# A causal convolution on TensorE: from groups of four phases to groups of eight, with the order of three engines written out by hand

## The chip, the core and the metric

The kernel runs on one core of one Trainium2 chip. A core has five engines that each take their instructions in order: TensorE (PE; its weight loads are listed as PEld), VectorE (DVE), ScalarE (ACT), GpSimd (POOL) and SyncE (SP). SP does no arithmetic here: it issues DMA transfers. ACT and POOL can issue DMAs too, and such an issue stands in the same queue as their computation. The metric is the device time of one execution in microseconds (us). Less is better.

## The reference: what is computed

The input `x` has 2 batches of 16000 tokens with 144 channels, in bf16. Fifteen taps at a distance of two tokens, each a 144 x 288 matrix, make a causal convolution; half of its 288 outputs goes through a tanh, the other half through a sigmoid, the product is multiplied by a 144 x 144 matrix.

```python
pad = (K - 1) * dil                       # K = 15, dil = 2
xp = jnp.pad(x, ((0, 0), (pad, 0), (0, 0)))
h = jnp.einsum('btc,cd->btd', xp[:, pad:pad + T, :], w[0])
for i in range(1, K):
    off = pad - i * dil
    h = h + jnp.einsum('btc,cd->btd', xp[:, off:off + T, :], w[i])
z = jnp.tanh(h[..., :D]) * _sigmoid(h[..., D:])
return z @ w_o
```

## The kernel before

**Layout.** TensorE contracts over at most 128 partitions, and there are 144 channels. So `x` is loaded transposed (channel on the partition, token along the row) in two pieces: `xn` holds channels 0 to 127, `xb` channels 16 to 143. The 16 channels left over (128 to 143) are copied out of `xb` eight times into one tile `rx`, each copy four tokens later than the one before. One matmul over `rx` so does the left-over channels of eight taps. Each batch is cut into chunks of 2048 tokens (16 chunks in all; the last of a batch is shorter). A chunk is loaded by `load_chunk` (L136): two transposing DMAs and eight copies, all on SP, with three buffers.

**Splitting over phases.** In the transposed layout a matmul takes 128 tokens with a step, as weights (`lhsT`), and the 288 outputs of one tap as the moving operand. Output tokens are sorted by their position modulo eight. A unit `unit_k4` (L334) makes four phases of 128 tokens each, at a step of eight: 512 tokens. It doesn't do fifteen taps for each of four phases. As in fast FIR algorithms it splits the filter into even and odd taps twice, and pays for fewer matmuls with sums: differences of the input (`en` = x shifted by 2 minus x, `fn` the same by 4, `gn` the same of `en` by 4) and of the weights (`s_main`, `ss`, `nso`, `aes`, `aos`, `nw2`) are made first. Then nine groups of four or five matmuls (41 in all, each 128x128 against 128x288) go to nine PSUM banks: `a1`, `a2`, `a3`, `c1`, `b1`, `b2`, `b3`, `c2`, `c3`. All matmuls are recorded on one line, L319 in `mm_group`. ACT copies `a1`, `c1` and `b1` to SBUF; DVE makes `q2 = a2 + a1`, `q3 = a3 + a1`, four sums `u0` to `u3` of two SBUF tiles (L360, L362, L368, L370), and four sums of a `u` with `b2`, `b3`, `c2`, `c3` (L373 to L382) into `y`.

**Gate and projection.** `gate` (L321) takes tanh and sigmoid on ACT and their product on DVE. Products go to DRAM (`zs_dram`), come back transposed as `zta` and `ztb` (72 channels each) by two transposing DMAs on SP, and `emit_outproj` (L299) multiplies them by the two halves of `w_o`: two matmuls with 144 columns for 128 tokens (L307, L308), copied out by ACT (L309). In the last chunk PE itself transposes (`emit_zside_pe`, L253). What 2048-token chunks leave over in a batch is done by `unit_k2` (two phases, 26 matmuls for 256 tokens) and `unit_std` (no splitting, 17 matmuls for 128 tokens).

**What sets the order.** The Tile scheduler orders the instructions of each engine; manual dependencies (`dma_T`, `dma_plain`) keep transposing and plain DMAs from running at the same time. Six PSUM banks serve the groups (`ps_acc`), two the projection (`ps_out`). The differences of the next chunk (`derive_steps`, each a DVE instruction over 2078 columns) are spread over the units of the present chunk, and so is the projection of the chunk before.

Of the kernel before, what the change touches and what calls it, by code (L numbers as in the profile page):

```python
# [15 lines left out]
def kernel(  # L16
# [6 lines left out]
):  # L23
    nc = tc.nc
    P = 128
    B, T, D = x.shape
    K = w.shape[0]
    D2 = w.shape[2]
    assert D2 == 2 * D and w.shape[1] == D
    CM = 128  # L30
    CR = D - CM
    assert CR == 16 and K == 15
    DH = D // 2
    KV = 8
    KO = 7
    NG = 8
    BOFF = D - P
    HTOK = 32
    assert T % P == 0 and T >= 4 * P
    dep_sync = mybir.DependencyInfo(mybir.DependencyClass.Sync, mybir.DependencyReason.DATA)  # L40
    dep_order = mybir.DependencyInfo(mybir.DependencyClass.NoSync, mybir.DependencyReason.SCHED_ONLY)

    KIND_TOK = {"k4": 8 * P, "k2": 4 * P, "std": P}

    def mk_items():
        items = []
        t = 0
        for kind in ("k4", "k2", "std"):
            n = KIND_TOK[kind]
            while T - t >= n:  # L50
                items.append((kind, t))
                t += n
        assert t == T
        return items

    CTOK = 2 * KIND_TOK["k4"]

    def mk_chunks():
        items = mk_items()
        groups = []  # L60
        i = 0
        while i < len(items):
            j = i
            span = 0
            while j < len(items) and span + KIND_TOK[items[j][0]] <= CTOK:
                span += KIND_TOK[items[j][0]]
                j += 1
            rest = sum(KIND_TOK[it[0]] for it in items[j:])
            if rest < KIND_TOK["k4"]:
                j = len(items)  # L70
            groups.append(items[i:j])
            i = j
        res = []
        for g in groups:
            t_a = g[0][1]
            t_b = g[-1][1] + KIND_TOK[g[-1][0]]
            res.append((g, t_a, t_b))
        return res

    def chunk_geom(t_a, t_b):  # L80
        if t_a == 0:
            R = min((t_b + 15) // 16 * 16, T)
            return R, 0, HTOK
        R = (t_b - t_a + HTOK + 15) // 16 * 16
        return R, t_b - R, 0

    chunk_list = mk_chunks()
    WB = 0
    SLOT = 0
    for (_, t_a, t_b) in chunk_list:  # L90
        R, t_lo, jlo = chunk_geom(t_a, t_b)
        assert t_lo >= 0 and t_lo + R <= T
        WB = max(WB, jlo + R)
        SLOT = max(SLOT, t_b - t_a)
    WB = (WB + 15) // 16 * 16
    SLOT = (SLOT + 15) // 16 * 16
    ZPAD = 16
    all_chunks = [(b, items, t_a, t_b) for b in range(B) for (items, t_a, t_b) in chunk_list]
    NCH = len(all_chunks)

    const = ctx.enter_context(tc.tile_pool(name="const", bufs=1))
    xa_pool = ctx.enter_context(tc.tile_pool(name="xa", bufs=3))
    xd_pool = ctx.enter_context(tc.tile_pool(name="xd", bufs=2))
    cp_pool = ctx.enter_context(tc.tile_pool(name="cp", bufs=3))
    y_pool = ctx.enter_context(tc.tile_pool(name="y", bufs=3))
    act_pool = ctx.enter_context(tc.tile_pool(name="act", bufs=2))
    z_pool = ctx.enter_context(tc.tile_pool(name="z", bufs=4))
    zt_pool = ctx.enter_context(tc.tile_pool(name="zt", bufs=2))
    os_pool = ctx.enter_context(tc.tile_pool(name="os", bufs=4))
    ztd_pool = ctx.enter_context(tc.tile_pool(name="ztd", bufs=2))  # L110
    ps_acc = ctx.enter_context(tc.tile_pool(name="ps_acc", bufs=6, space=bass.MemoryType.PSUM))
    ps_out = ctx.enter_context(tc.tile_pool(name="ps_out", bufs=2, space=bass.MemoryType.PSUM))
    dram = ctx.enter_context(tc.tile_pool(name="dram", bufs=1, space=bass.MemoryType.DRAM))

    fence_plain = []
    last_T = [None]

    def dma_T(out_ap, in_ap):
        ti = nc.sync.dma_start_transpose(out=out_ap, in_=in_ap)  # L119
        for prev in fence_plain:  # L120
            tc.add_manual_dep(ti.ins, prev, dep_sync, reason="dma batching")
        fence_plain.clear()
        if last_T[0] is not None:
            tc.add_manual_dep(ti.ins, last_T[0], dep_order, reason="dma batching")
        last_T[0] = ti.ins.name
        return ti

    def dma_plain(eng, out_ap, in_ap, track=True):
        di = eng.dma_start(out=out_ap, in_=in_ap)  # L129
        if last_T[0] is not None:  # L130
            tc.add_manual_dep(di.ins, last_T[0], dep_sync, reason="dma batching")
        if track:
            fence_plain.append(di.ins.name)
        return di

    def load_chunk(ci, cp_eng):  # L136
        b, items, t_a, t_b = all_chunks[ci]
        R, t_lo, jlo = chunk_geom(t_a, t_b)
        xn = xa_pool.tile([P, WB], BF16, name="xn")
        xb = xa_pool.tile([P, WB], BF16, name="xb")  # L140
        rx = xa_pool.tile([P, WB], BF16, name="rx")
        wv = jlo + R
        if jlo > 0:
            nc.gpsimd.memset(xn[:, 0:jlo], 0.0)
            nc.gpsimd.memset(xb[:, 0:jlo], 0.0)
        nc.gpsimd.memset(rx[:, 0:HTOK], 0.0)  # L146
        for (dst, c0) in ((xn, 0), (xb, BOFF)):
            src = bass.AP(x.tensor, x[b, t_lo, c0].offset, [[D, R], [1, P]])
            dma_T(dst[:, jlo:jlo + R], src)
        engs = cp_eng if isinstance(cp_eng, list) else [cp_eng]  # L150
        lasts = {}
        for g in range(NG):
            e_ = engs[g % len(engs)]
            lasts[id(e_)] = dma_plain(e_, rx[g * CR:(g + 1) * CR, 4 * g:wv], xb[P - CR:P, 0:wv - 4 * g],
                                      track=False)
        for l_ in lasts.values():
            fence_plain.append(l_.ins.name)
        return dict(xn=xn, rx=rx, joff=jlo - t_lo, wv=wv, has_k4=any(it[0] == "k4" for it in items))

    def derive_steps(cur):  # L160
        xn, rx, wv = cur["xn"], cur["rx"], cur["wv"]
        steps = []

        def s_en():
            en = xd_pool.tile([P, WB], BF16, name="en")
            nc.vector.tensor_tensor(out=en[:, 0:wv - 2], in0=xn[:, 2:wv], in1=xn[:, 0:wv - 2], op=ALU.subtract)  # L166
            cur["en"] = en

        def s_re():
            re = xd_pool.tile([P, WB], BF16, name="re")  # L170
            nc.vector.tensor_tensor(out=re[:, 0:wv - 2], in0=rx[:, 2:wv], in1=rx[:, 0:wv - 2], op=ALU.subtract)  # L171
            cur["re"] = re

        def s_fn():
            fn = xd_pool.tile([P, WB], BF16, name="fn")
            nc.vector.tensor_tensor(out=fn[:, 0:wv - 4], in0=xn[:, 4:wv], in1=xn[:, 0:wv - 4], op=ALU.subtract)  # L176
            cur["fn"] = fn

        def s_gn():
            en = cur["en"]  # L180
            gn = xd_pool.tile([P, WB], BF16, name="gn")
            nc.vector.tensor_tensor(out=gn[:, 0:wv - 6], in0=en[:, 4:wv - 2], in1=en[:, 0:wv - 6], op=ALU.subtract)  # L182
            cur["gn"] = gn

        steps = [s_en, s_fn, s_gn, s_re] if cur["has_k4"] else [s_en, s_re]
        cur["derived"] = True
        return steps

    def derive_chunk(cur):
        for f in derive_steps(cur):  # L190
            f()

    loaded = {}

    def ensure_chunk(ci, cp_eng=None):
        if ci < NCH and ci not in loaded:
            loaded[ci] = load_chunk(ci, cp_eng or nc.sync)

    w_all = const.tile([CM, K, D2], BF16)
    for qi, (t0, t1) in enumerate(((0, 4), (4, 8), (8, 12), (12, K))):  # L200
        dma_plain([nc.sync, nc.scalar][qi % 2], w_all[:, t0:t1, :], w[t0:t1, 0:CM, :].rearrange("k c d -> c k d"))

    def W(i):
        return w_all[:, i, :]

    ident = const.tile([P, P], BF16)
    make_identity(nc, ident[:])

    warm = const.tile([P, 1], F32)
    nc.gpsimd.memset(warm[:], 0.0)  # L210
    nc.scalar.activation(out=warm[:], in_=warm[:], func=ACT.Sigmoid)

    we_r = const.tile([NG * CR, D2], BF16)
    wo_p = const.tile([KO * CR, D2], BF16)
    dma_plain(nc.scalar, we_r[:], w[0:K:2, CM:D, :])
    dma_plain(nc.scalar, wo_p[:], w[1:K:2, CM:D, :])
    wo_sb = const.tile([DH, 2, D], BF16)
    dma_plain(nc.sync, wo_sb[:], w_o.rearrange("(h r) e -> r h e", h=2))

    zs_dram = dram.tile([NCH, SLOT + ZPAD, D], BF16, name="zs_dram")  # L220
    zpad_sb = const.tile([NCH, ZPAD * D], BF16)
    nc.gpsimd.memset(zpad_sb[:], 0.0)
    dma_plain(nc.sync, zs_dram[:, SLOT:SLOT + ZPAD, :].rearrange("c r d -> c (r d)"), zpad_sb[:])
# [29 lines left out]
    def emit_zside_pe(z_ap, ne, dst_ap):  # L253
        ps = ps_acc.tile([P, 512], F32, name="zt_ps", tag="acc")[0:DH, :].bitcast(BF16).rearrange(
            "p (e h m) -> p e h m", e=2, h=2)[:, :, :, 0:P]
        for e in range(ne):
            for h in range(2):
                nc.tensor.transpose(ps[:, e, h, :], z_ap(e)[:, h * DH:(h + 1) * DH], ident[:])  # L258
# [258 lines left out]
```

## Time and profile before

| | before |
|---|---|
| time, median of 3 runs (lowest to highest) | 390.22 us (389.55 to 390.4) |
| profiled execution: span from first to last instruction | 387.7 us |
| time that the page gives beside the span | none; the median of the runs is 2.5 us above the span |
| PE busy | 364.3 us, 3124 matmuls |
| DVE busy | 331.1 us, 753 instructions |
| ACT busy | 189.4 us, 448 instructions |
| POOL busy | 4.7 us, 28 instructions |
| moved by DMA | 60.27 MB, mean 155 GB/s |

Busy time counts the computing instructions of an engine from their start to their end; ends of matmuls are modelled, and one matmul overlaps the next, so that a mean duration (286 ns for 288 columns) says less than the distance between two starts. A group of instructions is given as line, engine, operation, `out<-in`, shapes, count, total busy time and mean duration of one; behind the bar stands how long the engine sat idle just before them, and for what. `L319` is line 319 of the kernel above. `ACTq` and `SPq` are issues of DMAs by these queues.

### The profile page before, as it was taken

To read this page: it belongs to the slowest core of one execution; us is meant where nothing else is said; L and a number is where in the kernel's file an instruction comes from. 1 tells how busy PE (TensorE), PEld (TensorE's weight loads), DVE (VectorE), ACT (ScalarE), POOL (GpSimd) and SP (SyncE) were. 2 spreads that over 40 slices of the span, in tenths; PEclk is the share of its full clock that TensorE was granted. 3 is DMA by queue.
4 is the path that set the end of the run, shared out by engine and by line. 5 is a ranking of instruction groups with operands and counts; after the bars stand their busy time and mean duration, and the time that the engine had idled before them with its cause. 6 is when DMAs were issued, how large, how long until landed. Compare 5 with 4: busy or idle time off the path is not lost.

```text
span 387.7 us, 8354 instructions
## 1 busy us (share of the span) xinstructions
PE 364.3 (94%) x3124; PEld 354.1 (91%) x3124; DVE 331.1 (85%) x753; ACT 189.4 (49%) x448; POOL 4.7 (1%) x28
## 2 busy tenths in 40 slices
PE   0669999999999999999999999999999999999995
PEld 0468998999999999999989999999999999999984
DVE  3489999998989999899859989999898989897651
ACT  4223445446454644546444454546545454654544
POOL 3000000000000000000000000000000000000000
PEclk9999999999999999999999999999999999999998
DMA  5865794596858859598798979696877969590602
GB/s 154 141 124 104 153 188 87 149 213 170 182 150 156 165 164 191 161 171 175 174 175 132 203 155 198 164 218 137 189 149 174 166 162 200 129 148 30 188 16 110
DMA packets 143475, 60.27 MB, mean 155 GB/s; under 512 B 131275, under 2 KB 133819, under 8 KB 143435
## 3 DMA queue, kind: packets, MB, share of 16 engines
q1 hardware_dynamic: 132764, 40.87, 58.7%
q10 hardware_dynamic: 10671, 18.88, 13.6%
q8 instruction: 24, 0.39, 0.4%
q14 instruction: 16, 0.13, 0.1%
HBM read 1.29 MB, written 18.03 MB: 50 GB/s over the span
## 4 chain that ended last, share of the span: by engine, by line
PE 71%; DVE 13%; DMA 5%; ACT 5%; issue 3%; ACTq 1%; SPq 1%; DVEq 0%
PE out_ps L307 4%; PE out_ps L308 3%; DMA xb<-in_x_dram 3%; ACT th L324 2%; ACTq L129 1%; DMA rx<-xb 1%; ACT sg L325 1%; PE v_ps L319 1%; DMA wo_p<-in_w_dram 1%; DVE en L166 1%; PE yo_ps L319 1%; DVE fn L176 1%; DVE re L171 1%; PE ye_ps L319 1%; SPq L119 1%
## 5 line engine op out<-in xcount | busy, mean ns | idle before, releaser
L319 PEld LDWEIGHTS <-gn 128*128 128x128 bf16 x900 | 116.0, 144 | 0.5 <-issue 0.3
L319 PEld LDWEIGHTS <-en 128*128 128x128 bf16 x540 | 67.0, 141 | 3.5 <-issue 2.6
L319 PEld LDWEIGHTS <-fn 128*128 128x128 bf16 x480 | 61.2, 144 | 2.6 <-DVE fn L176 1.8
L319 PEld LDWEIGHTS <-xn 128*128 128x128 bf16 x302 | 36.1, 136 | 13.6 <-DMA xn<-in_x_dram 11.8
L307 PE MATMUL out_ps<-wo_sb,zta 72*128 72x144 bf16 x237 | 38.7, 226 | 1.5 <-ACT os_2884 L309 0.7
L308 PE MATMUL out_ps<-wo_sb,ztb 72*128 72x144 bf16 x237 | 37.9, 227 | 0.0
L319 PEld LDWEIGHTS <-re 112*128 112x128 bf16 x248 | 35.3, 143 | 1.2 <-DVE re L171 1.1
L308 PEld LDWEIGHTS <-ztb 72*128 72x128 bf16 x237 | 31.4, 143 | 5.2 <-issue 2.3
L307 PEld LDWEIGHTS <-zta 72*128 72x128 bf16 x237 | 32.8, 144 | 0.1
L171 DVE TENSOR_TENSOR re<-rx 128x2078 bf16<-128x2078 bf16 (+1 forms) x16 | 19.3, 1206 | 5.8 <-DMA rx<-xb 5.8
L166 DVE TENSOR_TENSOR en<-xn 128x2078 bf16<-128x2078 bf16 (+1 forms) x16 | 19.3, 1205 | 1.9 <-DMA xn<-in_x_dram 1.9
L319 PEld LDWEIGHTS <-rx 128*128 128x128 bf16 (+1 forms) x128 | 18.0, 142 | 1.9 <-DMA rx<-xb 1.8
L182 DVE TENSOR_TENSOR gn<-en 128x2074 bf16<-128x2074 bf16 (+1 forms) x16 | 19.3, 1206 | 0.1
L176 DVE TENSOR_TENSOR fn<-xn 128x2076 bf16<-128x2076 bf16 (+1 forms) x16 | 19.3, 1204 | 0.0
L319 PE MATMUL a_192<-ss,xn 128*128 128x288 bf16 x4 | 1.2, 447 | 11.8 <-DMA xn<-in_x_dram 11.8
L229 DVE COPY s_main<-w_all 128x288 bf16<-128x288 bf16 x1 | 0.2, 234 | 6.6 <-DMA w_all<-in_w_dram 6.6
L260 DVE COPY zt_sb<-zt_ps 72x512 bf16<-72x512 bf16 (+1 forms) x7 | 2.6, 394 | 3.7 <-PE zt_ps L258 3.7
L146 POOL MEMSET rx<- 128x32 bf16 x16 | 1.8, 122 | 302.3 <-PE a_449 L319 33.3
L319 PE MATMUL v_ps<-s_main,xn 128*128 128x288 bf16 x32 | 4.7, 286 | 0.0
L319 PE MATMUL h_ps<-w_all,xn 128*128 128x288 bf16 x30 | 4.7, 286 | 0.0
L319 PE MATMUL yo_ps<-w_all,en 128*128 128x288 bf16 x32 | 4.6, 286 | 0.0
L319 PE MATMUL ye_ps<-wo_neg,en 128*128 128x288 bf16 x28 | 4.4, 286 | 0.0
(1922 smaller groups left out, 987.8 us busy)
## 6 DMA issues: line engine op xcount, KB each, us to landing
rx<-xb SPq DMA_DIRECT2D x14, 65.0 KB, 2.7
rx<-xb SPq DMA_DIRECT2D x14, 64.8 KB, 2.6
rx<-xb SPq DMA_DIRECT2D x14, 64.5 KB, 4.0
rx<-xb SPq DMA_DIRECT2D x14, 64.2 KB, 2.8
rx<-xb SPq DMA_DIRECT2D x13, 64.9 KB, 2.9
rx<-xb SPq DMA_DIRECT2D x13, 64.6 KB, 2.6
rx<-xb SPq DMA_DIRECT2D x13, 64.4 KB, 3.0
rx<-xb SPq DMA_DIRECT2D x13, 64.1 KB, 3.2
```

The costliest lines, as they stand in the source:

```text
L119: ti = nc.sync.dma_start_transpose(out=out_ap, in_=in_ap)
L129: di = eng.dma_start(out=out_ap, in_=in_ap)
L166: nc.vector.tensor_tensor(out=en[:, 0:wv - 2], in0=xn[:, 2:wv], in1=xn[:, 0:wv - 2], op=ALU.subtract)
L171: nc.vector.tensor_tensor(out=re[:, 0:wv - 2], in0=rx[:, 2:wv], in1=rx[:, 0:wv - 2], op=ALU.subtract)
L176: nc.vector.tensor_tensor(out=fn[:, 0:wv - 4], in0=xn[:, 4:wv], in1=xn[:, 0:wv - 4], op=ALU.subtract)
L182: nc.vector.tensor_tensor(out=gn[:, 0:wv - 6], in0=en[:, 4:wv - 2], in1=en[:, 0:wv - 6], op=ALU.subtract)
L260: nc.vector.tensor_copy(out=sb[:, 0:ne], in_=ps[:, 0:ne])
L307: nc.tensor.matmul(po[:, e, :], lhsT=ck["zta"][0:DH, sl], rhs=wo_sb[:, 0, :], start=True, stop=False)
L308: nc.tensor.matmul(po[:, e, :], lhsT=ck["ztb"][0:DH, sl], rhs=wo_sb[:, 1, :], start=False, stop=True)
L319: nc.tensor.matmul(ps[:, 0:D2], lhsT=l, rhs=r, start=(i == 0), stop=(i == n - 1))
L324: nc.scalar.activation(out=th[:, 0:ne, :], in_=y_ap[:, :, 0:D], func=ACT.Tanh)
L325: nc.scalar.activation(out=sg[:, 0:ne, :], in_=y_ap[:, :, D:D2], func=ACT.Sigmoid)
```

## The change

The convolution, the gate and the projection are written anew. The pieces:

- **Windows and octets.** Each batch is cut into 8 windows of 2000 tokens, of which each is computed as 2048 (128 rows of 16 phases), so there is one kind of unit. A window makes two octets (`rho` 0 and 1): eight phases of 128 tokens at a step of 16. There are 32 octets, and neither `unit_k2` nor `unit_std`.
- **A third level of splitting.** The five groups `A1`, `A2`, `A3`, `B1`, `C1` (class `Leaf`) are split over two phases each: `common` makes two matmuls, ACT copies that partial sum from one PSUM bank into a second one, and `private` accumulates two matmuls on top in either bank (of difference tiles `d8`, `d48`, `d28`), `rest` one more where left-over channels belong. The four groups `b2`, `b3`, `c2`, `c3` (`direct`) are as before, done for two phases each. An octet has 34 matmuls of leaves and 38 of direct products, all with 288 columns.
- **Who adds.** The sums of two SBUF tiles (before: `u0` to `u3` on DVE) are on GpSimd, four per octet, each over two phases (128 x 576 values, fp32), written into `y`. DVE adds `b2` to `c3` from PSUM onto `y`. It makes `q2`, `q3` as before.
- **Input differences.** Seven instead of four per window. Four of the seven (`d8`, `d4`, `d48`, `d28`) only make the columns that are read: runs of 2 or 4 with gaps.
- **Products and projection.** Products are stored as `zm` (channels 0 to 127 of eight phases) and `zr` (the other 16 channels of eight phases side by side). The projection makes three groups of PSUM per octet, each one matmul of the left-over channels of two or three phases against a block-diagonal `wo_bd` and one matmul with 144 columns per phase. Two stores per octet are issued on ACT, two transposing loads on SP; the projection lags two octets.
- **Order.** PE, ACT and DVE run in the order in which the program is written. In the loop the leaves of octet n+1 lie between the direct products of octet n, the gate's second half of octet n-1 and the projection of octet n-2. Five PSUM banks are for leaves and three for direct products and projection. Input tiles have two buffers instead of three; window w+2 is loaded into the buffers of w.
- **Start.** Twenty matmuls over zeros run first; all four loads of `w_all` are on ACT, behind the load of its function table; three small weight loads and three preparations of weights are on GpSimd.

The core of the diff (of the removed side only the tails that the text speaks of; the functions themselves are printed above):

```diff
-        u1 = cp_pool.tile([P, D2], F32, name="u1")
-        nc.vector.tensor_tensor(out=u1[:], in0=c1s[:], in1=q2[:], op=ALU.add)
...
-        mm_group(c3, [(st(gn, -8 * j), W(4 * j)) for j in range(4)] + [(st(re, 4), we_r[:])])
-        nc.vector.tensor_tensor(out=y_sb[:, 3, :], in0=c3[:, 0:D2], in1=u3[:], op=ALU.add)
...
+        return [sub("d8", "x", 8, 0, 8, 2), sub("d4", "x", 4, 0, 4, 2), sub("d48", "d4", 8, 0, 4, 2),
+                sub("d2", "x", 2), sub("d28", "d2", 8, 6, 8, 4), sub("d24", "d2", 4), sub("re", "rx", 2)]
...
+    warm = const.tile([P, 1], F32)
+    nc.vector.memset(warm[:], 0.0)
+    nc.scalar.activation(out=warm[:], in_=warm[:], func=ACT.Sigmoid)
+    zero = const.tile([P, 512], BF16)
+    nc.vector.memset(zero[:], 0.0)
+    for i in range(NWARM):
+        t = ps_leaf.tile([P, 512], F32, name="lf", tag="lf")
+        nc.tensor.matmul(t[:], lhsT=zero[:, 0:P], rhs=zero[:], start=True, stop=True)
...
+    add(bc[:], wq[:, :, 0], wq[:, :, 1], nc.gpsimd)
...
+        def common(self):
+            sig, dsig, off, v, e, o, rem = self.a
+            self.ts = [bank(), bank()]
+            for j in range(2):
+                mm(self.ts[0], st(sig, off - 16 * j), v(j), j == 0, j == 1)
+            nc.scalar.copy(out=self.ts[1][:, 0:D2], in_=self.ts[0][:, 0:D2])
+
+        def private(self, i):
+            sig, dsig, off, v, e, o, rem = self.a
+            f, o_ = ((e, off - 8), (o, off))[i]
+            for j in range(2):
+                mm(self.ts[i], st(dsig, o_ - 16 * j), f(j), False, rem is None and j == 1, True)
...
+        def eoBC(self, leaf, name, u, v, op):
+            t = self.new(name)
+            for i in range(2):
+                leaf.private(i)
+                nc.scalar.copy(out=t[:, i, :], in_=leaf.rest(i)[:, 0:D2])
+            for k, q in ((u, self.q2), (v, self.q3)):
+                nc.gpsimd.tensor_tensor(out=self.y[:, k::4, :], in0=q[:], in1=t[:], op=op)
+
+        def direct(self, k, off, f, n, rem, op, phases):
+            d24 = self.s["d24"]
+            rsig, roff, rw, rows = rem
+            for i in phases:
+                ps = ps_dir.tile([P, 512], F32, name="dir", tag="dir")
+                for j in range(n):
+                    mm(ps, st(d24, off + 8 * i - 8 * j), f(j), j == 0, False)
+                mm(ps, st(rsig, roff + 8 * i, rows), rw, False, True)
+                nc.vector.tensor_tensor(out=self.y[:, k + 4 * i, :], in0=self.y[:, k + 4 * i, :], in1=ps[:, 0:D2], op=op)
...
+    def z_by_dma(slot, zm, zr):
+        zt = zt_pool.tile([P, 9, P], BF16, name="zt")
+        nc.scalar.dma_start(out=zm_dram[slot], in_=zm[:].rearrange("p r c -> p (r c)"))
+        nc.scalar.dma_start(out=zr_dram[slot], in_=zr[:].rearrange("p r c -> p (r c)"))
+        nc.sync.dma_start_transpose(out=zt[:, 0:8, :], in_=zm_dram[slot])
+        nc.sync.dma_start_transpose(out=zt[:, 8, :], in_=zr_dram[slot])
+        return zt
...
+        if o:
+            o.A1.common()
+        if d:
+            d.b2()
+        if o:
+            o.A2.common()
+            o.eoA1()
+        if p:
+            p.act(1)
+        if d:
+            d.b3((0,))
+        if o:
+            o.A3.common()
+            o.eoA(o.A2, "q2", ALU.subtract)
+        if d:
+            d.b3((1,))
+        if p:
+            p.mult(1)
+        if o:
+            o.B1.common()
+            o.eoA(o.A3, "q3", ALU.add)
+        if p:
+            z_side(n - 1)
+        pre()
+        if d:
+            d.c2((0,))
+        project()
+        if d:
+            d.act(0)
+            d.c2((1,))
+        pre()
+        if o:
+            o.C1.common()
+            o.eoBC(o.B1, "b1s", 0, 2, ALU.subtract)
+        project()
+        if d:
+            d.c3((0,))
+            d.mult(0)
+        if o:
+            o.eoBC(o.C1, "c1s", 1, 3, ALU.add)
+        pre()
+        if d:
+            d.c3((1,))
+        project()
+        pre()
```

Here `o` is octet n+1, `d` octet n, `p` octet n-1; `pre()` emits one input difference of the next window, `project()` one group of the projection of octet n-2, `act` the tanh and sigmoid of four phases, `mult` their two products (`zm` and `zr`), `eoA1` the `private` parts of `A1` with a copy of each to SBUF, `eoA` those of `A2` or `A3` with the DVE sum into `q2` or `q3`.

## The prediction

> **What bounds the kernel now.** I read the page's table of engines first, then the chain of work that ended last, then busy time by stretch, and then one unit of the steady part in the timeline. All times are in us.
>
> ```profile
> PE 364.3 (94%) x3124; PEld 354.1 (91%) x3124; DVE 331.1 (85%) x753; ACT 189.4 (49%) x448; POOL 4.7 (1%) x28
> ...
> PE 71%; DVE 13%; DMA 5%; ACT 5%; issue 3%; ACTq 1%; SPq 1%; DVEq 0%
> ```
>
> PE is busy nearly always and carries 71% of the chain. DVE, with 85%, is close behind; ACT has half its time free, POOL nearly all.
>
> ```profile
> 0.00:23.11 23.11, 7.50 (x41) 5.53 (x42) 9.10 (x14) 7.00 (x9) 2.97 (x13) 1.00 0.65 133
> 23.11:200.00 176.89, 174.06 (x1483) 169.83 (x1482) 164.44 (x370) 86.70 (x205) 1.11 (x10) 1.00 0.77 162
> 200.00:360.00 160.00, 159.35 (x1385) 157.64 (x1384) 144.31 (x335) 82.74 (x200) 0.62 (x5) 1.00 0.76 161
> 380.70:387.70 7.00, 2.92 (x36) 2.27 (x33) 1.18 (x4) 3.00 (x10) 0.00 (x0) 0.86 0.30 111
> ```
>
> The columns are: stretch, length, busy time (and count) of PE, PEld, DVE, ACT, POOL, then clock, DMA share, GB/s. The start of 23.1 does only 41 matmuls' work, the tail of 7.0 next to none. Between them the granted clock is full and PE works.
>
> ```profile
> 205.61 0.65 PE L319 MATMUL a_3321<-ss,xn 128*128 128x288 bf16 x4
> 205.89 0.45 DVE L373 TENSOR_TENSOR y_3243<-b_3289,u_3285 128x288 f32<-128x288 f32 x1
> 206.25 0.45 DVE L376 TENSOR_TENSOR y_3243<-b_3295,u_3287 128x288 f32<-128x288 f32 x1
> ...
> 207.46 0.69 ACT L324 ACTIVATE th<-y_3243 128x576 bf16<-128x576 f32 x1 [0.76 <-DVE y_3243 L382]
> ...
> 208.06 0.67 ACT L325 ACTIVATE sg<-y_3243 128x576 bf16<-128x576 f32 x1
> ...
> 210.64 0.65 PE L319 MATMUL a_3401<-ss,xn 128*128 128x288 bf16 x4
> ```
>
> From `a_3321` to `a_3401` a unit of 41 matmuls takes 5.03: 0.1227 per 288-column matmul. What counts is this distance of starts, not the mean duration. In the same way DVE takes 0.37 for a sum over 288 values, ACT 0.60 for 576, and ACT copies of 288 stand 0.30 apart (`c1s` to `b1s`). PE's 144-column projections stand 0.0625 apart.
>
> **PE's work, before and after.** Before: 2598 matmuls of 288 columns (per batch 30 x 41 + 2 x 26 + 17) x 0.1227 = 318.8, 500 of 144 columns x 0.0625 = 31.3, transposes 2: 352 in all. After: 32 octets x 72 x 0.1227 = 282.7; projection per octet 8 x 0.0625 plus 1152 columns at the 288-column rate (0.49), 0.99 x 32 = 31.7. In all 314.4: 38 less, or 9.82 per octet. The octets' 2.4% of tokens computed twice are in it. Weights read at a step of 16 cost the same, I assume: steps of 1, 4 and 8 all show 0.122 to 0.123 here, and a weight load fits into the 0.0625 of a projection matmul. A clear loss would show as longer distances.
>
> **Start.** Before, PE's first matmul waits to 11.85 for `xn` and the second unit starts at 23.11. After, `xb` and `xn` are issued first on SP; `xn` landed 4.2 after its issue here, so it is there at about 8. The four loads of `w_all` now queue on ACT behind the table load (1.28), 0.55 an issue, and landed after 4.2 to 4.5: about 7.5 to 10. Then DVE does 14 preparations: at 1.15 for 2078 values (0.554 ns each) and about 0.07 apiece they add to 9.6, ending at 17 to 19.5. Four `q` sums (1.5) and the round trip of `B1` and `C1` over ACT (2) follow: the loop starts at 20.5 to 23, I take 22. By then the 34 leaf matmuls of octet 0 are done (4.2 of the 314.4). The upper end is 27, if POOL's `bc` (2304 values; 5.1 at the rate below) holds DVE up all the while. The twenty matmuls over zeros end before 12 even at the distance of 0.245 per 288 columns that the first four matmuls of the profile show, in time in which PE waits anyway.
>
> **Tail.** After the last direct product: DVE 0.45, tanh and sigmoid 1.3, products 0.55, nine transposes and three DVE copies (0.41 each) 1.5, six projection groups with ACT copies 2.5, issue and landing of one store of 590 KB (288 KB took 2.1 to 4.3): about 10. Bounds: 7, as before, and 13.
>
> So with PE never waiting in the loop: 22 + 310.2 + 10 = 342 of span. The page gives the profiled execution its span alone, 387.7; the median of the runs, 390.22, is 2.5 above it, and with that I get 345. Each us that PE waits per octet adds 32. Call it s: **time = 344.7 + 32 s**.
>
> **What s holds, per octet of 9.82.** ACT: 11 copies x 0.30, 4 gate halves x 0.60, projection copies 1.2, 2.5 DMA issues x 0.34: 7.75. DVE: 12 sums x 0.37 = 4.44, products 0.88, differences (3.5 per octet; 4930 values x 0.554) 2.73: 8.05. If runs of 2 or 4 go at half that rate, 1815 values cost 1.0 more: 9.05. Before, DVE had 10.4 per 1024 tokens (two units of 11 x 0.37, four differences of 1.15 to every four units), 3.0 of it in the eight `u` sums that move to POOL. So DVE has 1.77 to spare.
>
> POOL: four sums of 576 values. No sum of tiles ran on POOL, so two rows bound it: 2304 values were set in 2.01, which gives 0.50 for 576; the selection of 128x128 in `ident` took 0.28, which gives 1.27. I take 1.27, since it reads and writes SBUF as a sum does and the other only writes. 5.1 per octet fits into 9.82. A sum written after `B1`'s copies, at about 9.0, ends at 10.3; its first reader is `b2`'s add in the next octet at 10.7.
>
> The trace never shows POOL reading SBUF while DVE works. If neither holds up the other, the loss c on DVE is 0 (a gain is excluded: nothing of DVE gets shorter). If each sum holds up one DVE instruction by its whole length, c is 5.1. DVE's instructions that work on SBUF alone (products, differences) are 3.6 of its 8.05, or 45%; that share of 5.1 is 2.3. I take c = 2.3: 0.5 over the slack of 1.77.
>
> The Trainium skill ("SBUF — State Buffer", section "Who interferes with whom") states that a DVE instruction with two SBUF inputs and a GpSimd instruction that reads SBUF exclude each other for whole instructions. No row here shows it. It speaks against this change: taken at its hardest, with c = 5.1, s would be 3.3 and the time 450; by the trace's rows alone c may as well be 0.
>
> ACT has a chain of its own. Counting from an octet's start, PE ends the first projection group at 6.15; ACT copies it until 6.85, then does `act(0)` until 8.1, then `C1`'s bank copy until 8.6; PE wants `C1`'s private matmuls at 8.45. That is a wait of 0.2. Queued in front on ACT are the two stores of `z_side`, which wait for DVE's `mult(1)` (done at 5.2): if DVE is a us late there, PE is too. This overlaps with DVE's lateness; together I take **s = 0.5**.
>
> **Moved steps with one answer each.** SP per window: two loads (2.1 each), eight `rx` copies (6.9 to 8.0), two long and two short transposes (half of 2.1 and less): 15 of 20.6; before, 16 of 22. The load of window w+2 is queued behind the `A1` matmuls of w and lands some 6 later; DVE reads it 15 after. Without that cover every us of lateness would hold DVE up once per window, 0.5 on s. A product's way through DRAM (store landing 2 to 4, transpose 4) is 8 of the 10.4 that two octets of lag leave.
>
> **The sum.** 344.7 + 32 x 0.5 = 361, against 390.2: 29 less, of 38 that PE saves.
>
> **Rivals.**
> - *PE alone bounds:* c below 1.8, ACT's chain in time: 343 to 349. For it: PE waited only 0.65 in the stretch from 200 to 360. Against: then one engine had slack; now DVE, ACT and PE all stand at 79 to 100%.
> - *DVE becomes the bound without deciding the sign:* strided differences at half rate (9.05) with c of 1.7 to 2.1, s = 0.9 to 1.4: 373 to 389. For it: no row shows a difference over short runs. Against: 3.0 of sums has left DVE.
> - *POOL's sums decide, slower than before:* between `mult(0)` and the next `mult(1)` the sums run back to back, and every product and difference there waits for one. From c = 3.2 (63% of the sums' time) s passes 1.42 and the gain is gone. At c = 3.8, three sums of four, s = 2.0: 409; at the end 450. For it: four of DVE's eight SBUF-only instructions lie in that stretch. Against: `c3` and `b2` adds read PSUM and lie between them.
> - *The change doesn't do what it says:* excluded for the count of matmuls; for POOL, the same as the one above.
>
> **How the numbers follow.** Forecast 0.52 (349 to 373), PE alone 0.13, DVE in between 0.13, POOL decides 0.18, below 343 0.02, and 0.02 within 0.2% of the time before, about what a measurement of this kernel can tell from no change. Faster: 0.80; slower: 0.18. The range from 343 to 386 leaves out the slower cases and holds 0.8. The start's upper end (+5) and the tail's (+3) lie inside.
>
> **What the new profile would show.** PE: 2685 matmuls with 288 columns still 0.123 apart; the loop from about 22; 10.3 per octet. POOL sums of 1.27, and products or differences on DVE longer than 0.37 and 1.23, or late, just where a sum runs. PE's waits named after `C1`'s copy or after DVE's adds. I am wrong if POOL's sums take 2 and more, if distances of matmuls grow with the step of 16, or if the wait of an octet sits on a DMA.

## The result, and the profile after

The changed kernel takes **445.6 us** (444.69 and 446.45; two further runs took 461.35 and 468.87) against 389.88 beside it: slower, by a factor of **1.143 [1.140, 1.146]**. The profiled execution took 444.69, with a span of 442.9. Runs more than 1.5% above the fastest of the same kernel are left out of every time and ratio here, and as the traces of e4 and e11 come from such runs, only single rows of them are read.

First the page's table of engines and its chain, to be held against 94%, 85%, 49%, 1% and a chain of 71% PE:

```profile
PE 346.3 (78%) x2685; PEld 315.5 (71%) x2685; DVE 376.4 (85%) x636; ACT 238.2 (54%) x581; POOL 231.4 (52%) x163
...
PE 41%; DVE 33%; issue 10%; DMA 8%; ACT 4%; SPq 1%; POOL 1%; DVEq 0%; ACTq 0%
```

PE has fewer matmuls, as planned, and is no longer what ends last. DVE has 117 instructions fewer than before and is busy 45 us longer; POOL's sums are busy 213 us (104.3 + 109.1 below) where 128 sums of 1.27 would have made 163. Busy time by stretch (columns as before: stretch, length, PE, PEld, DVE, ACT, POOL, clock, DMA share, GB/s):

```profile
0.00:37.92 37.92, 14.97 (x55) 7.89 (x56) 21.22 (x20) 7.97 (x15) 17.93 (x20) 0.70 0.73 133
37.92:424.50 386.58, 326.05 (x2598) 304.11 (x2597) 352.94 (x609) 225.74 (x558) 213.48 (x144) 0.98 0.71 125
424.50:442.90 18.40, 5.27 (x35) 3.46 (x33) 2.22 (x9) 4.45 (x9) 0.00 (x0) 0.69 0.25 79
```

All three stretches are longer than forecast: start 37.9 for 22, loop 386.6 for 326 (310.2 + 16), tail 18.4 for 10. The loop is 12.08 per octet. Where its time goes is seen in one stretch of the timeline (start, length, engine, line, instruction):

```profile
199.18 0.42 DVE L307 TENSOR_TENSOR zm<-th,sg 128x512 bf16<-128x512 bf16 x1
199.28 2.98 POOL L270 TENSOR_TENSOR y<-q,b1s 128x576 f32<-128x576 f32 x2 [3.85 <-issue]
199.52 1.42 DVE L308 TENSOR_TENSOR zr<-th,sg 128x64 bf16<-128x64 bf16 x1
200.85 2.50 DVE L107 TENSOR_TENSOR re<-rx 128x2078 bf16<-128x2078 bf16 x1
202.21 3.81 POOL L270 TENSOR_TENSOR y<-q,c1s 128x576 f32<-128x576 f32 x2
203.27 1.17 DVE L280 TENSOR_TENSOR y<-y,dir 128x288 f32<-128x288 f32 x3
203.77 0.65 PE L195 MATMUL dir<-w_all,d 128*128 128x288 bf16 x4 [1.71 <-DVE y L280]
204.25 0.29 PE L195 MATMUL dir<-wo_p,re 112*128 112x288 bf16 x1
...
206.88 0.19 DVE L308 TENSOR_TENSOR zr<-th,sg 128x64 bf16<-128x64 bf16 x1
```

The product `zr` covers 64 values a partition. With no sum on POOL it takes 0.19 (last line); begun beside the first sum it takes 1.42 and ends when that sum is over. `re` then takes 2.50 (1.23 where nothing runs beside it), since the second sum got in first, and PE waits 1.71 for the adds queued behind them on DVE. DVE's adds from PSUM never grow (0.43 to 0.48 in all 256).

A long wait of PE costs more than its length. The longest of the loop, 4.43, ends at 55.42; two stretches behind it (columns as above):

```profile
55.40:59.50 4.10, 4.08 (x18) 2.82 (x18) 3.12 (x6) 1.65 (x3) 0.00 (x0) 0.50 0.00 0
59.50:64.00 4.50, 4.50 (x38) 4.50 (x37) 4.12 (x11) 2.87 (x8) 0.22 (x1) 1.00 0.20 67
```

At a granted clock of 0.50 PE starts a matmul of 288 columns every 0.24, at 1.00 every 0.12. Over the loop the clock is 0.98, where the kernel before had 1.00.

The groups of the whole run (busy us, mean ns | idle before):

```profile
L270 POOL TENSOR_TENSOR y<-q,b1s 128x576 f32<-128x576 f32 x64 | 104.3, 1651 | 148.1 <-ACT b1s L268 72.6
L270 POOL TENSOR_TENSOR y<-q,c1s 128x576 f32<-128x576 f32 x64 | 109.1, 1723 | 0.0
L307 DVE TENSOR_TENSOR zm<-th,sg 128x512 bf16<-128x512 bf16 x64 | 49.7, 776 | 1.8 <-ACT sg L303 1.8
L308 DVE TENSOR_TENSOR zr<-th,sg 128x64 bf16<-128x64 bf16 x64 | 42.4, 662 | 0.0
L107 DVE TENSOR_TENSOR re<-rx 128x2078 bf16<-128x2078 bf16 x16 | 32.3, 2021 | 0.0
```

The start shows the same thing once, with longer instructions:

```profile
12.87 4.53 POOL L115 TENSOR_TENSOR bc<-w_all 128x2304 bf16<-128x2304 bf16 x1 [7.51 <-DMA w_all<-in_w_dram]
13.51 4.97 DVE L107 TENSOR_TENSOR d<-xn 128x518 bf16<-128x518 bf16 x2 [12.33 <-DMA xn<-in_x_dram]
...
24.65 6.63 POOL L159 TENSOR_SCALAR wn<-w_all 128x2304 bf16<-128x2304 bf16 x1
25.30 6.62 DVE L107 TENSOR_TENSOR d<-d 128x2074 bf16<-128x2074 bf16 x1
```

Two differences that take 1.22 without POOL (e4, e8) take 4.97 beside `bc`, and one of 1.24 takes 6.62 beside `wn`: 9 us lost. Besides, `xn` landed only at 13.4 (8 was assumed).

### The profile page after: what moved, and what is told of

The parts are those of the page before. It is cut to its first block, busy times and chain, and to the rows that moved or that the text cites. A ratio compares the mean times of both kernels' runs of the same rounds, so it can differ in the third digit from the quotient of the medians.

```text
span 442.9 us, 7858 instructions
## 1 busy us (share of the span) xinstructions
PE 346.3 (78%) x2685; PEld 315.5 (71%) x2685; DVE 376.4 (85%) x636; ACT 238.2 (54%) x581; POOL 231.4 (52%) x163
## 4 chain that ended last, share of the span: by engine, by line
PE 41%; DVE 33%; issue 10%; DMA 8%; ACT 4%; SPq 1%; POOL 1%; DVEq 0%; ACTq 0%
PE dir L195 19%; PE lf L195 18%; DVE d L107 8%; DVE y L280 8%; DVE zm L307 5%; DVE q L262 5%; DVE zr L308 4%; DMA zt<-zr_dram 3%; DVE re L107 3%; DMA xn<-in_x_dram 3%; PE po L336 2%; PE po L339 2%; DMA zm_dram<-zm 1%; ACT th L302 1%; ACT sg L303 1%
## 5 line engine op out<-in xcount | busy, mean ns | idle before, releaser
L195 PEld LDWEIGHTS <-d 128*128 128x128 bf16 x1856 | 237.5, 145 | 76.5 <-issue 70.8
L270 POOL TENSOR_TENSOR y<-q,b1s 128x576 f32<-128x576 f32 x64 | 104.3, 1651 | 148.1 <-ACT b1s L268 72.6
L280 DVE TENSOR_TENSOR y<-y,dir 128x288 f32<-128x288 f32 x256 | 108.8, 447 | 33.8 <-PE dir L195 25.7
L195 PE MATMUL dir<-w_all,d 128*128 128x288 bf16 x512 | 86.8, 294 | 47.7 <-DVE y L280 47.7
L270 POOL TENSOR_TENSOR y<-q,c1s 128x576 f32<-128x576 f32 x64 | 109.1, 1723 | 0.0
L215 ACT COPY lf<-lf 128x288 f32<-128x288 f32 x160 | 62.6, 391 | 78.6 <-PE lf L195 49.5
L195 PE MATMUL dir<-wn,d 128*128 128x288 bf16 x448 | 75.5, 289 | 5.2 <-DVE y L280 5.2
L107 DVE TENSOR_TENSOR d<-xn 128x518 bf16<-128x518 bf16 (+2 forms) x48 | 58.1, 1214 | 12.3 <-DMA xn<-in_x_dram 12.3
L107 DVE TENSOR_TENSOR d<-d 128x1034 bf16<-128x1034 bf16 (+2 forms) x48 | 58.4, 1219 | 0.1
L262 DVE TENSOR_TENSOR q<-a1s,lf 128x288 f32<-128x288 f32 x128 | 52.1, 447 | 3.3 <-PE lf L195 2.7
L195 PE MATMUL dir<-wo_p,re 112*128 112x288 bf16 x128 | 37.9, 296 | 0.0
L107 DVE TENSOR_TENSOR re<-rx 128x2078 bf16<-128x2078 bf16 x16 | 32.3, 2021 | 0.0
```

What stands on the lines that cost most here:

```text
L107: eng.tensor_tensor(out=o, in0=a, in1=b_, op=ALU.subtract)
L195: nc.tensor.matmul(ps[:, 0:D2], lhsT=l, rhs=r, start=start, stop=stop, skip_group_check=on)
L215: nc.scalar.copy(out=self.ts[1][:, 0:D2], in_=self.ts[0][:, 0:D2])
L262: nc.vector.tensor_tensor(out=q[:, i, :], in0=self.a1s[:, i, :], in1=leaf.rest(i)[:, 0:D2], op=op)
L270: nc.gpsimd.tensor_tensor(out=self.y[:, k::4, :], in0=q[:], in1=t[:], op=op)
L280: nc.vector.tensor_tensor(out=self.y[:, k + 4 * i, :], in0=self.y[:, k + 4 * i, :], in1=ps[:, 0:D2], op=op)
```

## The experiments

Two theories were set against each other first. EXCLUSION: a POOL instruction that reads SBUF and a DVE instruction with two SBUF inputs keep each other out for their whole length. ORDER: POOL is a bystander, and it is the order of the work that makes PE wait. "Loop" below is the distance from the first to the last start of a direct matmul divided by 32 (12.06 for the change); "loads" is the time of all 32 transposing loads of x in SP's queue, "us" the median of the runs that count (2 as a rule, 6 for e15, 5 for e12, one for e2, e4, e9 and e11). e1, e2, e5 and e6 leave the sums out and don't compute the result; they are there to find causes.

| kernel | us | loop | loads | PE waits for DVE's `y` | PE waits for `zt` |
|---|---|---|---|---|---|
| the change | 445.6 | 12.06 | 138.9 | 52.9 | 6.0 |
| e1 sums replaced by memsets | 430.4 | 11.46 | 146.7 | 1.5 | 40.4 |
| e2 sums replaced by copies | 427.4 | 11.46 | 148.2 | 10.2 | 28.9 |
| e3 sums on DVE, fp32 | 442.9 | 11.94 | 143.0 | 49.9 | 5.2 |
| e4 preparations off POOL | 448.5 | - | - | - | - |
| e5 e1, stores issued by POOL | 385.2 | 10.17 | 97.2 | 1.3 | 11.0 |
| e6 e5 with fences | 481.4 | 13.22 | 82.0 | 1.3 | 24.5 |
| e7 e8 with fences | 464.8 | 13.08 | 72.2 | 3.1 | 57.9 |
| e8 bf16 sums on DVE, stores by POOL | 369.3 | 10.17 | 104.1 | 3.0 | 4.6 |
| e9 e8, sums back on POOL | 464.9 | 13.17 | 76.5 | 78.3 | 0 |
| e10 e8, stores by ACT | 411.1 | 11.46 | 140.3 | 2.7 | 32.3 |
| e11 the change, stores by POOL | 463.7 | - | - | - | - |
| e12 e8 with another start | 373.6 | 10.38 | 102.9 | 3.1 | 8.2 |
| e13 e8, idle reads on POOL | 456.5 | 12.90 | 95.7 | 75.0 | 0 |
| e14 e8, idle memsets on POOL | 369.2 | 10.20 | 107.8 | 3.1 | 5.3 |
| e15 e8 again | 369.8 | 10.16 | 104.2 | 3.0 | 4.3 |

### e1 and e2: what POOL reads

```diff
-nc.gpsimd.tensor_tensor(out=self.y[:, k::4, :], in0=q[:], in1=t[:], op=op)
+nc.gpsimd.memset(self.y[:, k::4, :], 0.0)             # e1
+nc.gpsimd.tensor_copy(out=self.y[:, k::4, :], in_=t[:])   # e2
```

> The four POOL sums of an octet are left out: in their place POOL only fills the same values of y with zeros (y so lacks q2, q3, b1 and c1). POOL keeps as many instructions, writing as much into the same tiles, but reads nothing. Theory EXCLUSION (a POOL instruction that reads SBUF and a DVE instruction with two SBUF inputs keep each other out for whole instructions): products and differences go back to their own lengths (zr 0.19, zm 0.42, differences 0.35 to 1.23 us), the loop falls from 386.6 to 320-330 us, start (38) and tail (18) stay, span 376 to 390 us instead of 442.9. Rival ORDER (DVE, ACT and PE are late because of the written order and the round trips between them, POOL is a bystander): span 425 to 445.

> The four POOL sums of an octet are left out: POOL copies b1s or c1s into y instead, one SBUF input in place of two. EXCLUSION: a read is a read; POOL's instruction gets shorter (about 0.6 to 0.8 us), each still holds a product or a difference up for its whole length, so about half of the loss goes: span 395 to 415 us. If only POOL instructions with two inputs exclude DVE: 376 to 390, as without any read. ORDER: 425 to 445.

The DVE side came as EXCLUSION had it. In e1 POOL writes the same values for 0.58 each and reads nothing (groups of e1):

```profile
L307 DVE TENSOR_TENSOR zm<-th,sg 128x512 bf16<-128x512 bf16 x64 | 26.8, 418 | 2.0 <-ACT sg L303 2.0
L308 DVE TENSOR_TENSOR zr<-th,sg 128x64 bf16<-128x64 bf16 x64 | 11.8, 184 | 0.0
L107 DVE TENSOR_TENSOR re<-rx 128x2078 bf16<-128x2078 bf16 x16 | 19.7, 1232 | 0.0
```

Not one `zr` is over 0.19. Against the change `zm` lost 22.9, `zr` 30.6, `re` 12.6 and the other differences 25.0 us: 91 in all, 2.85 per octet. In e2 POOL's copies have one input (0.66 alone), and `zr` grows to at most 0.655: a read of one tile is enough, and what it costs goes by its own length. But both times missed: the span of e1 is 425.9, where EXCLUSION had 376 to 390, that of e2 425.6 (395 to 415). By its time alone e1 even came out as ORDER had it. PE's waits for DVE had fallen from 52.9 to 1.5 and 10.2, and waits of 40.4 and 28.9 for `zt`, the products back from DRAM, stood in their place. There was a second bound close behind the first.

### e3: the sums on VectorE

```diff
-nc.gpsimd.tensor_tensor(out=self.y[:, k::4, :], in0=q[:], in1=t[:], op=op)
+nc.vector.tensor_tensor(out=self.y[:, k::4, :], in0=q[:], in1=t[:], op=op)
```

> The four sums of an octet are made by DVE instead of POOL, at the same place in its order, nothing is left out. EXCLUSION: DVE has 8.05 + 4 x 0.67 = 10.7 us per octet and nothing that holds it up: loop 345 to 360, span 400 to 416 us, less than with the sums on POOL though DVE does 86 us more work. ORDER: DVE is the late engine and gets 2.7 us per octet more: span 470 to 530.

Nothing is stretched (`zr` at most 0.193), but a sum of 576 fp32 values takes 0.75 on DVE, and DVE is busy 371.1: PE waits for it nearly as long as in the change (49.9), at 11.94 per octet. The span of 439.7 lies between what the two theories had. So the sums in fp32 fit neither engine: by DVE's busy time in e3 and e1, (371.1 - 290.8) / 32, the change had moved 2.5 us an octet off DVE, and by the same measure, (376.4 - 290.8) / 32, it lost 2.7 there.

### e4: the start alone

```diff
-add(bc[:], wq[:, :, 0], wq[:, :, 1], nc.gpsimd)
-neg(ns_r[:], s_r[:], nc.gpsimd)
-neg(wn[:], wq[:, :, 1], nc.gpsimd)
+add(bc[:], wq[:, :, 0], wq[:, :, 1])     # VectorE
+neg(ns_r[:], s_r[:])                     # ScalarE
+neg(wn[:], wq[:, :, 1])
```

> Only the start: the three preparations of weights on POOL go to DVE (bc) and ACT (ns_r, wn); the sums of the loop stay on POOL. EXCLUSION: d8 and d4 (4.97 us together behind bc, 1.0 alone) and d24 (6.62 behind wn, 1.15 alone) get their own lengths, bc costs DVE 1.3: the loop starts 7 to 9 us sooner, at 29 to 31 instead of 37.9, span 433 to 437 us. ORDER: the start stays at 37 to 40 and the span at 441 to 445.

The first direct matmul starts at 31.7 instead of 38.4, with the differences back at 1.22 for two and 1.23. In the whole time this gain isn't seen (448.5 against 445.6), and where it went stays open.

### e5, e6: the second bound

In e1 SP's queue is full. Its rows for one window (157.81 to the next load of `xb` at 179.42, two octets):

```profile
157.81 5.60 SPq L84 DMA_TRANSPOSE xb<-in_x_dram  x1
163.50 5.08 SPq L84 DMA_TRANSPOSE xn<-in_x_dram  x1
168.67 1.17 SPq L86 DMA_DIRECT2D rx<-xb  x2
169.94 1.28 SPq L317 DMA_TRANSPOSE zt<-zm_dram  x1
171.31 1.50 SPq L318 DMA_TRANSPOSE zt<-zr_dram  x1
172.87 3.75 SPq L86 DMA_DIRECT2D rx<-xb  x6
176.71 1.27 SPq L317 DMA_TRANSPOSE zt<-zm_dram  x1
178.08 1.18 SPq L318 DMA_TRANSPOSE zt<-zr_dram  x1
179.42 7.31 SPq L84 DMA_TRANSPOSE xb<-in_x_dram  x1
```

The two loads take 10.7, where the kernel before needed 2.1 for each (median of its 32), and the products of an octet wait behind them. Two causes were possible: the change had dropped the fences `dma_T` and `dma_plain` that kept transposing and plain DMAs apart (FENCE), or there is just too much in the queue (QUEUE). e5 lets POOL issue the stores and is the partner of e6, which adds the fences.

```diff
-nc.scalar.dma_start(out=zm_dram[slot], in_=...)     # and zr_dram, out
+nc.gpsimd.dma_start(out=zm_dram[slot], in_=...)     # e5
+dma_plain(nc.gpsimd, zm_dram[slot], ...)            # e6; loads and zt by dma_T
```

> Leaves out the sums (the memset of e1 in their place) and lets GpSimd's queue issue the stores of z and of the output instead of ScalarE's; nothing else. It is the partner of the next kernel. Both theories on what bounded e1 (FENCE: the transposing loads of x are slow because plain DMAs are in flight beside them; QUEUE: there is simply too much work in SP's queue) expect what e1 gave: 424 to 437 us, xb and xn loads with medians of 5 to 7 us, waits of PE on zt 30 to 45 us. If it lies under 415, ScalarE's issues had delayed z and were a part of the cause.

> As e5, and with the two DMA helpers of the kernel before, which make every transposing load wait until the plain DMAs issued ahead of it have landed and every plain DMA wait for the last transposing load; the output's store is issued ahead of the next window's loads. FENCE expects xb and xn back at 2.0 to 2.3 us each, the waits of PE on zt under 15 us, a period of 9.8 to 10.4 us per octet and 375 to 405 us. QUEUE expects loads that stay at 4 us and more, or a queue that is longer by the added waits, and 425 us or more.

On e5 both theories missed. Meant as a control, it gained 45 us: its loads take 97 instead of 147 us in all, PE waits 11.0 for `zt`, and the loop is 10.17. The fences of e6 do make loads shorter still (82), but SP then waits for the landing of what stands before them (75.4 for `zm_dram`, 40.4 for `zr_dram`, 34.8 for `rx`), as QUEUE had said of e6. The loads so come late: DVE waits 88.6 for `xn`, PE another 56.6 for PSUM banks that DVE's adds have to free, and the loop is 13.22. What e5 changed is the queue that issues the stores; but the scheduler of SP's queue also put one `rx` copy ahead of the products where e1 has two, so e10 below repeats the step.

### e7, e8, e10: removing both bounds

e8 does all the work. The sums are on DVE with bf16 tiles (`q2`, `q3`, `b1s`, `c1s` and the sums are rounded to bf16: 0.45 each, for 0.75 in fp32 in e3) and behind the next direct product; POOL issues the stores; `bc`, `ns_r`, `wn` are off POOL; the weights are issued first, on SP and ACT ahead of the table load, and `xn` ahead of `xb`; PE transposes the products of the last two octets. e7 is e8 with the fences and the output's store ahead of the loads, e10 is e8 with the stores on ACT.

```diff
-nc.gpsimd.tensor_tensor(out=self.y[:, k::4, :], in0=q[:], in1=t[:], op=op)
+nc.vector.tensor_tensor(out=self.ys[:, k::4, :], in0=q[:], in1=t[:], op=op)  # bf16
...
-if i == NO - 1:
+if i >= NO - 2:
     o.zt = z_by_pe(zm, zr)
```

> All the work is done. The sums are on VectorE again, on bf16 tiles (q2, q3, b1s, c1s and the sums are rounded to bf16) and laid behind the next direct product; the preparations of weights are off GpSimd; stores are issued by GpSimd; the fences of e6; weights and the first window are loaded in the order of need; the products of the last two octets are transposed by PE. If EXCLUSION and FENCE are both the causes, nothing is stretched (zr at most 0.25 us), DVE has 7.4 + 4 x 0.45 = 9.2 to 9.8 us per octet, under PE's 9.84 or at it: loop 315 to 330, start 25 to 30, tail 10 to 14, so 355 to 380 us. If QUEUE is right, the waits of PE on zt remain at 20 us and more: 395 to 430.

> As e7 without the fences and with the output's store behind the loads as in the change. FENCE expects the loads of x at 5 to 7 us again, PE waiting for zt 25 us and more, 390 to 425 us, at least 15 us over e7. QUEUE expects it within 5 us of e7 or under it.

> As e8, with the stores of z and of the output issued by ScalarE's queue again, as in the change. If the queue of the stores is the second bound, the pair of loads of x takes 8 to 9.5 us again (e8: 6.6 by the medians), PE waits 20 us and more for zt (e8: 4.6) and the time is 395 to 425 us. If e8 was fast for its other parts, it stays under 375.

e8 takes **369.3 us**, faster than both kernels. e7 takes 464.8, far above what either theory had for it: the fences cost 95 us, though the loads are nearly as short as in the kernel before (2.2 each by the median, 2.1 there). That plain DMAs beside them lengthen the loads agrees with this; that fences make the kernel faster is refuted. e10 against e8 differs in the queue of the stores (SP's order differs in one place only) and takes 411.1, with PE waiting 32.3 for `zt`. The time that the packets of SP's queue take, as a share of 16 engines' span, first of e8 (span 366.7) and then of e10 (408.6):

```profile
q1 hardware_dynamic: 109344, 34.96, 54.9%
q0 software_dynamic: 5792, 18.24, 17.5%
```

```profile
q1 hardware_dynamic: 109344, 34.96, 63.9%
q10 hardware_dynamic: 11648, 18.58, 14.7%
```

The same 109,344 packets take 201 us of 16 engines in e8 and 261 in e10, 1.3 times as long. The bytes stored are equal; issued by POOL they are 5,792 packets, by ACT about 10,700 (11,648 less the 928 of weights that ACT issues in e8 too). A late issue is not the cause: by the median, ACT in e10 issues the store of `zm` as its product ends and POOL in e8 0.2 later, but the transpose that brings it back starts in SP's queue 5.8 behind the product in e10 and 3.6 in e8. So the second bound is 11.46 an octet in e1, e2 and e10 alike, and the store's queue sets it. Why loads are slower beside stores in that queue isn't settled; the smaller packets are only a candidate. The Trainium skill ("DMA: Bandwidth & Descriptors", section "Issuing engine by pattern") gives simple stores to SyncE and calls DMAs issued there or by ScalarE generally faster than GpSimd's. For a store by itself no run here decides that; beside transposing loads, GpSimd's issue was worth 42 us (e10 against e8).

### e9, e11: the sums back on GpSimd

```diff
-nc.vector.tensor_tensor(out=self.ys[:, k::4, :], in0=q[:], in1=t[:], op=op)
+nc.gpsimd.tensor_tensor(out=self.y[:, k::4, :], in0=q[:], in1=t[:], op=op)   # e9, fp32
```

> As e8 (stores issued by GpSimd, preparations off GpSimd, order of the first loads, the last two octets transposed by PE), all the work done, but the sums are on GpSimd in fp32 at the place where the change has them. PE had 10.0 us per octet in e8 with VectorE busy 10.0. EXCLUSION (an instruction of GpSimd that reads SBUF and one of VectorE that reads two SBUF inputs keep each other out) expects zr again at up to 1.4 us and a period of 11 to 12.1 us per octet: 26.5 + 32 x 11 to 12.1 + 14 = 393 to 428 us, at least 25 us over e8, although VectorE has 1.65 us per octet less of its own to do. ORDER (GpSimd is a bystander; the stores and the start were what cost) expects 360 to 370 us.

> The change with one thing undone: the stores are issued by GpSimd, sums stay on GpSimd in fp32. With e1, e5 and the change this closes a square (sums there or not, stores on ScalarE or GpSimd: 444.7, this, 430, 385). If the two bounds lie behind one another, EXCLUSION holds the loop at 11.5 to 12.1 us and the time at 425 to 445, a gain of less than 20 where e5 gained 45 over e1. If the costs simply add, it is 395 to 403.

464.9 and 463.7: slower than either theory had it, slower than the change itself. Here POOL's queue holds the sums behind stores that wait for `zr` (87.5 us in e9), so exclusion and queue are mixed, and neither run tells them apart. DVE's busy time speaks for exclusion: 394.3 in e9, 104 more than in e5, where nothing on POOL reads in the loop; the change has 86 more than e1. What e11 does show is that the costs of the change don't add: moving the stores to POOL gains 45 us without sums there (e1 to e5), and loses 18 with them.

### e13, e14: exclusion by itself

Both add work on POOL to e8, behind the stores of z, whose result nobody reads. The order of all other engines, SP's queue included, is e8's.

```diff
 z_side(n - 1)
+for _ in range(4):                                       # e13
+    nc.gpsimd.tensor_tensor(out=da[:], in0=p.zm[:, 0:4, :], in1=p.zm[:, 4:8, :], op=ALU.add)
+nc.gpsimd.tensor_copy(out=da[:, 0, 0:1], in_=p.zr[:, 7, 0:1])   # e14
+for _ in range(10):
+    nc.gpsimd.memset(da[:], 0.0)
```

> e8 with four additions of bf16 halves of zm on GpSimd per octet (128 x 512, two inputs in SBUF, result read by nobody), issued behind the stores of z; no other engine's order changes and no engine waits for them, but zm is held longer by one of three buffers. About 4.5 to 5.5 us of GpSimd per octet. EXCLUSION expects zr stretched from 0.19 to 1.1 us and more, VectorE from 10.0 to 11.5 to 14 us per octet and 415 to 490 us. ORDER or QUEUE (what cost was that others wait for GpSimd's queue) expects 366 to 374 us.

> The control for e13: a copy of one column of zr and ten memsets (128 x 512 fp32, about 0.5 us each, no input) on GpSimd per octet at the same place, again some 5 us of GpSimd per octet for which nobody waits. EXCLUSION and ORDER both expect e8's time, 366 to 374 us, and zr at 0.19; only if a busy queue of GpSimd (stores behind the memsets) is itself the cost does it go with e13.

**456.5 against 369.2 us**. The page's table of engines, first of e13 (span 457.3) and then of e14 (368.9):

```profile
PE 355.8 (78%) x2694; PEld 320.5 (70%) x2694; DVE 405.3 (89%) x768; ACT 241.2 (53%) x583; POOL 217.8 (48%) x232
PE 334.1 (91%) x2694; PEld 311.9 (85%) x2694; DVE 321.0 (87%) x768; ACT 237.5 (64%) x583; POOL 217.0 (59%) x449
```

POOL is busy equally long. DVE is busy 84 us more for the same 768 instructions, and the span is 88 longer. Only SP ever waits for POOL's queue (for the memset in `rx`, 12.2 us in e13 and 3.8 in e14), and PE's waits for `zt` are 0 and 5.3 (e8: 4.6), so that cost e13 nothing. One stretch of e13:

```profile
232.46 5.51 POOL L460 TENSOR_TENSOR da<-zm 128x512 f32<-128x512 bf16 x4
234.92 0.58 DVE L314 TENSOR_TENSOR zm<-th,sg 128x512 bf16<-128x512 bf16 x1
235.43 1.15 DVE L315 TENSOR_TENSOR zr<-th,sg 128x64 bf16<-128x64 bf16 x1
236.50 1.78 DVE L277 TENSOR_TENSOR ys<-q,b1s 128x576 bf16<-128x576 bf16 x2
```

and PE's longest wait in e13, 75.0 us in 48 pieces, is on those adds:

```profile
PE dir L196 <- DVE y L287: 75.0, 48, 3.3
```

ORDER is refuted: no engine is ordered otherwise than in e8.

### e12 and e15: a better version

```diff
-neg(an[:], quad[:, :, 1])       # ScalarE, all ahead of the first copy
-neg(ns_r[:], s_r[:])
-neg(wn[:], wq[:, :, 1])
 o.A1.common()
+neg(an[:], quad[:, :, 1])       # and ns_r, wn further down
```

> e8 with ScalarE's preparations of weights laid behind its first copies out of PSUM (in e8 PE waits 6.0 us for the first of these behind them, and 1.6 for bcn), and bc behind the first differences. The loop is e8's. Start 4 to 6 us sooner: 362 to 367 us.

> e8 again, in five rounds: 367 to 371 us, a ratio to the kernel before of 0.942 to 0.953.

e12 takes 373.6, slower than e8. It starts its direct products at 24.9 instead of 26.3 and then loses 6.7 in the loop. One load of `xn` now stands behind the first products of z in SP's queue, and PE waits 8.2 for `zt` instead of 4.6; that is half of it. Much of the rest lies behind the longest of these waits, 5.06 up to 78.01: from 78 to 84 the granted clock is 0.55 and PE starts 30 matmuls, in the next 6 us 51. e15 repeats e8 in five rounds: 369.8 us, a ratio to the kernel before of **0.948 [0.945, 0.951]**, 20 us faster.

## Why the prediction was wrong

The forecast was 361 with 0.80 for faster; what came true is the rival "POOL's sums decide, slower than before", which had 0.18 and prices of 409 to 450.

- **PE's work: right.** 2685 matmuls; the step of 16 costs nothing (four matmuls from 203.77 to 204.25 are 0.12 apart). Where both bounds are gone the loop is 10.16 (e15), against 9.82 for PE alone.
- **Differences over short runs: right but for one.** In e8, with nothing beside them, 1032 to 1038 values in runs of 2 or 4 at twice that step take 0.70 and 2078 in one run 1.23, so nearly the same rate. Only `d8`, 518 values in runs of 2 at a step of 8, takes 0.66, about half the rate; that is 0.1 per octet, and the rival fell.
- **POOL's sum: nearly right in its undisturbed size.** Taken at 1.27, the shortest is 1.39. But POOL is held up by DVE as well, and the means are 1.65 and 1.72.
- **The failed step is "c = 2.3: 0.5 over the slack of 1.77".** Two things in it. c measured 2.85. Compared one by one with e1, 81 of DVE's instructions are longer, by 1.1 each; that is 63 for every 100 sums, where 45% had been taken, a share of DVE's time for the chance of a meeting. But a sum runs where a product is made: `zr` of `mult(0)` was stretched in 25 of 32 octets, that of `mult(1)` in none. This size alone would have moved the forecast by 18 us (0.55 x 32). And the slack couldn't be used in full. s came out at (386.6 - 310.2) / 32 = 2.39, not 0.5, where c of 2.85 over the slack of 1.77, with the 0.2 of ACT's chain, would be 1.28. PE's waits for DVE's adds alone are 52.9 / 32 = 1.65. A stretch comes in lumps of 1.2, or 2.5 for two in a row, at one place, ahead of the adds that free the three direct banks, and PE stands still there; slack elsewhere in the octet gives only a part of that back. Another 0.5 an octet is PE's own work, busy 326.1 us for the 310.2 of the forecast, some of it at half the clock behind a wait; the sum had nothing for that.
- **Where the 84 us lie.** The forecast had a span of 358.2, measured are 442.9: 60 us more in the loop, 16 in the start, 8 in the tail. (The 2.5 added to the span is 1.8 in this execution, 444.69 for 442.9.) The rule from "SBUF — State Buffer", section "Who interferes with whom", agrees with e13, e14 and the stretched rows (0.19 to 1.42). That its price at the hardest, 450, is near the 445.6 is luck: c was 2.85 and not 5.1, and 24 us are start and tail.
- **Start: 22 taken, upper end 27, measured 37.9.** `bc` did hold DVE up, but so did `wn`, which wasn't priced: 9 us together. And `xn` came at 13.4; up to there the DMA engines were busy all the time (share 1.00, 191 GB/s) with weights and x together. With both mended e8 starts at 26.3.
- **Tail: 10 taken, 7 to 13; measured 18.4.** Only the last octet goes by PE; the products of octet 30 still go through DRAM, and PE waits for them until 431. The way of 8 was put against two octets of lag, which the last iteration doesn't give.
- **"SP per window: two loads (2.1 each)" was wrong,** and it would have cost the gain by itself: the durations were those of another arrangement, with the stores kept apart by fences. Here they are 4.3 on average. In the change this bound lies hidden, as far as e1 shows it: take the sums' reads away and the loop goes from 12.06 to 11.46 and no further.

The forecast of 361 was not out of reach: e8 keeps the third level of splitting and takes 369.

## What to carry to other kernels

Before a sum of SBUF tiles goes to GpSimd, count which VectorE instructions with two SBUF inputs can run beside it; each meeting can cost up to the whole length of the other instruction, however short its own work is, and the engine that is freed of 2.5 us can lose 2.7. A duration of a DMA holds for what else is in flight, so a change that moves stores to another queue or drops fences needs its loads priced anew. When a repair gains less than it should, look for the next bound (here 12.06, 11.46, 10.17 an octet) instead of doubting the first cause.

## What the hardware showed that wasn't expected

- A POOL instruction with one SBUF input excludes DVE as well: copies of 0.66 stretched `zr` to 0.655 (e2), and a negation on POOL (`wn`, 6.63) held a difference of 1.24 for 6.62. Memsets excluded nothing, 164 us of them (e14, 310 of 0.53).
- PE's long waits cost twice: behind the waits of 4.43 (the change) and 5.06 (e12) the granted clock was 0.50 and 0.55 for 4 and 6 us, and matmuls took twice the distance. In e8, where PE waits at most 1.91 in the loop, the clock of the loop is 1.00.
- Transposing loads of x took 140 us of SP's queue when ACT issued the stores and 104 when POOL did, for the same bytes.
- Keeping transposing and plain DMAs apart made the loads shorter (72 against 104 us, e7 and e8) and the kernel 95 us slower.
